# One load each for w_up and wo, all heads normalized at once, and w_down cut at half rows 16 and 24, in a decode kernel on one core

## The chip, the cores and the metric

The kernel runs on one core of one Trainium2 chip. The metric is the device time of one execution in microseconds (us); lower is better. The core has a matmul engine (TensorE, PE in the profile, its weight loads as PEld), VectorE (DVE), ScalarE (ACT), GpSimd (POOL) and SyncE (SP), which here issues nearly all DMAs. Sixteen DMA engines serve the core.

## The reference

One token passes through an attention block and a gated MLP, in bfloat16. All weights and caches are read once.

```python
# D = 640, Hq = Hkv = 32, Sk = 4096, Dh = 128, Df = 1728; B = S = 1
def _A_ref(x, k_cache, v_cache, wq, wo):            # x is layernormed
    q = (x @ wq)                                    # [640] -> 32 heads x 128
    scores = einsum("bhqd,bhkd->bhqk", q, k_cache) * (Dh ** -0.5)
    p = softmax(scores)
    o = einsum("bhqk,bhkd->bhqd", p, v_cache)
    return o.reshape(B, Sq, Hq * Dh) @ wo           # [4096] -> [640]

def _B_ref(x, w_gate, w_up, w_down):                # x is layernormed
    return (gelu(x @ w_gate) * (x @ w_up)) @ w_down # 640 -> 1728 -> 640

h  = x + _A_ref(layernorm(x), k_cache, v_cache, wq, wo)
h2 = h + _B_ref(layernorm(h), w_gate, w_up, w_down)
```

The key and value caches are 33.5 MB each, the weights 17 MB together: 84.2 MB in all.

## The kernel before, in words

The instructions of each engine are written out by hand. A small class (`Prog`) keeps one list per engine in program order and turns the dependencies given with each operation into semaphore waits. There is no scheduler: an engine runs its list in order, and where its next operation waits, all behind it wait too. SP issues every load from one list, so the loads also queue in program order on the same 16 DMA engines.

**Attention.** The 32 heads are handled in four groups `G` of 8. A group's keys come as one 8.4 MB load to one of three slots: 128 partitions, 16 for each head, with 256 keys each. The values come the same way. The order is K0, V0, K1, V1, K2, K3, V2, V3, and a slot is loaded again when its reader is done. For each group, eight times (`c`): VectorE multiplies keys with the query (`score_mult`, L310), PE folds the products with eight identity matmuls (L318 and L30), VectorE sums (`score_sum`, L327). Then `softmax` (L332 to L341), `attend` (64 matmuls of probabilities with values, L353), and `pick` (L359 to L363), which brings the group's output to `po_r`. `head_sum` (L367, L369) adds over the 16 partitions of a head; its results collect in bank 4 (`ps_a`).

**Normalize, spread, take.** Heads go in two halves, `t`: `t=0` is groups 0 and 1, `t=1` groups 2 and 3. `normalize(t)` divides by the softmax sums (L373, L374), `spread(t)` is one matmul (L377) that lays 16 heads out over 128 partitions eight times, and `take(t)` keeps the wanted one of eight and adds up (L381, L386). The result, `aP[:, t, :]`, is a column for each of 16 rows of wo that a partition holds. For `t=0` this runs inside group 2's loop (at `c` = 4, 5 and 6), for `t=1` after the last `attend`.

**Projection.** wo comes in two loads, `d_wo[0]` and `d_wo[1]`, each 16 rows to a partition (20,480 bytes). `proj_part(t, lo, hi)` does two matmuls for each row (L398 and, with weights kept, L30), four rows side by side in 32-column strips of the array. All of `t=0` stands in PE's list ahead of `d_wo[1]`'s matmuls, woven between `head_sum(3)` and `spread(1)`.

**Tail.** The projected row is cast to a high and a low part (L471 to L473), turned to columns (L479), added to x and layernormed (L272 to L282, L488, L489). `glu` (L512) is 20 matmuls for the gate, then 20 for up: 12 on the first w_up load (`d_wu[0]`, three of five row blocks), 8 on the second. `turn` casts a row of results (L518, VectorE for the gate, ScalarE for up) and turns it to columns by six matmuls (L522, L524). VectorE and ScalarE compute gelu (L535 to L542) and the product `hm` (L545, L547). `down` is 54 matmuls (L555, L564), two for each of w_down's 27 half rows of 320 elements on 128 partitions; they come in three loads cut at `LOADS`. Two casts (L567) and the output DMA follow.

**Padding.** `run_on(n)` (L455, L30) puts n matmuls of an identity, 512 columns wide, into PE's list, whose result nobody reads. They stand at the places where PE would idle in the tail.

SP's list at the end, in order: wo (two loads, waiting for `attend(2)`), w_gate (waiting for group 3's last fold), w_up (two), w_down (three), output.

Of the kernel before, what the change touches and what calls it, by code (L numbers as in the profile page):

```python
# [5 lines left out]
FP32 = mybir.dt.float32  # L6
BF16 = mybir.dt.bfloat16
ALU = mybir.AluOpType
# [3 lines left out]
D = 640  # L12
# [10 lines left out]
PIECE = 320  # L23
LOADS = ((0, 19), (19, 25), (25, 27))

# [86 lines left out]
def bass_sequential_preLN__gqa_block_cached__glu_gated_geglu__decode_kernel(nc, A_x, A_k_cache, A_v_cache, A_wq, A_wo, B_x, B_w_gate, B_w_up, B_w_down, out):  # L112
# [16 lines left out]
    hlnT = sb("hlnT", [128, 5], BF16)  # L129
    rz = sb("rz", [16, 2], FP32)  # L130
    po_r = sb("po_r", [128, 2, DH + 1], FP32)
    m4 = sb("m4", [128, 4], FP32)
    hs = sb("hs", [128, 24], FP32)
    hb = sb("hb", [128, 24], FP32)
    hbx = sb("hbx", [128, 8, 4], BF16)
    aT = sb("aT", [16, 2, 128], BF16)
    aP = sb("aP", [128, 2, 16], BF16)
    sel = sb("sel", [16, 16, 8], BF16)
    m8 = sb("m8", [128, 8], FP32)
    aM = sb("aM", [128, 8, 16], FP32)  # L140
    sel4 = sb("sel4", [128, 4], BF16)
# [31 lines left out]
    hs_t = first_t.take(128).rearrange("p (a b c) -> p a b c", a=8, b=4)  # L173
    m8_t = first_t.take(128).rearrange("p (a b) -> p a b", a=8)
    par_t = first_t.take(128).rearrange("p (a b) -> p a b", a=2)
# [18 lines left out]
    wq_sb = slots[2][:, 0:5 * 4096]  # L194
    wo_sb = slots[0][:, 0:32 * D].rearrange("p (t i n) -> p t i n", t=2, i=16)
    wg_sb = slots[2][:, 0:5 * DF].rearrange("p (c n) -> p c n", c=5)
# [44 lines left out]
    c_bz = GP(lambda e: e.memset(hb[:, :], 0.0))  # L241
    c_hb = mask(hb[:, 8:16], ones_b[:, 0:8], [[-16, 8]], 0, 1, ALU.is_ge, c_bz)
    c_hb = mask(hb[:, 8:16], hb[:, 8:16], [[16, 8]], 15, -1, ALU.is_ge, c_hb)
    c_m4 = mask(m4_t, ones_b[:, 0:128].rearrange("p (a b) -> p a b", a=4), [[-1, 4], [-4, 32]], 0, 1, ALU.is_equal)
# [5 lines left out]
    c_hx = mask(hbx[:, :, :], hbx[:, :, :], [[16, 8], [0, 4]], 15, -1, ALU.is_ge, c_hx)  # L250
    c_sel = mask(sel[:, :, :], ones_b[0:16, 0:128].rearrange("p (a b) -> p a b", a=16), [[1, 16], [0, 8]], 0, -1, ALU.is_equal)
    c_m8 = mask(m8_t, ones_b[:, 0:128].rearrange("p (a b) -> p a b", a=8), [[-1, 8], [-8, 16]], 0, 1, ALU.is_equal)

    c_odd = V(lambda e: e.reduce_sum(odd[:, :], hb[:, 8:16].rearrange("p (a b) -> p b a", b=2), axis=AX.X), c_hb)
    c_far = V(lambda e: e.tensor_scalar(far[:, :, :], odd[:, :].unsqueeze(2).to_broadcast([128, 2, 16]), -1e38, 1e38, ALU.mult, ALU.add), c_odd)
    c_m4 = V(lambda e: e.reduce_sum(m4[:, :], m4_t, axis=AX.X), c_m4)
    c_m8 = V(lambda e: e.reduce_sum(m8[:, :], m8_t, axis=AX.X), c_m8)
    c_hs = V(lambda e: e.reduce_sum(hs[:, 8:16], hs_t.rearrange("p a b c -> p a (b c)"), axis=AX.X), c_hs, c_hz)
    c_o4 = V(lambda e: e.reduce_max(ones4[:, :], sel4[:, :], axis=AX.X), c_s4)
# [37 lines left out]
    q1 = V(lambda e: e.tensor_copy(qb[:, :, :].rearrange("p g d -> p (g d)"), ps_q[:, :]), qd)  # L297
    free2 = [qd, c_par, c_m4, c_m8, c_hs, c_idb]

    folds, reds, exps, pbs, pvs, mks, evs, hds, nbs = {}, {}, {}, {}, {}, {}, {}, {}, {}  # L300
    z4s, spr, aPs = {}, {}, {}
    held = [False]

    def other(fn, *d):
        held[0] = False
        return T(fn, *d)
# [58 lines left out]
    def head_sum(G):  # L365
        g, at = G % 2, 132 * (G // 2)
        other(lambda e: e.matmul(ps_a[0:16, at + DH:at + DH + 1], hb[:, 8 - 8 * g:24 - 8 * g], po_r[:, g, DH:DH + 1],  # L367
                                 start=(g == 0), stop=(g == 1), skip_group_check=True), exps[G], z4s.get(G // 2 - 1), c_hb)
        hds[G] = T(lambda e: e.matmul(ps_a[0:16, at:at + DH], hs[:, 8 - 8 * g:24 - 8 * g], po_r[:, g, 0:DH],  # L369
                                      start=False, stop=(g == 1), skip_group_check=True), evs[G], c_hs)  # L370

    def normalize(t):
        rc = V(lambda e: e.reciprocal(rz[:, t:t + 1], ps_a[0:16, 132 * t + DH:132 * t + DH + 1]), hds[2 * t + 1])  # L373
        z4s[t] = V(lambda e: e.tensor_scalar(aT[:, t, :], ps_a[0:16, 132 * t:132 * t + DH], rz[:, t:t + 1], None, ALU.mult), rc)  # L374

    def spread(t):
        spr[t] = other(lambda e: e.matmul(ps_z[:, 32:160], sel[:, :, :].rearrange("p a b -> p (a b)"), aT[:, t, :], start=True, stop=True),  # L377
                       z4s[t], c_sel)

    def take(t):  # L380
        m = V(lambda e: e.tensor_tensor(out=aM[:, :, :], in0=ps_z[:, 32:160].rearrange("p (q i) -> p q i", q=8),  # L381
                                        in1=m8[:, :].unsqueeze(2).to_broadcast([128, 8, 16]), op=ALU.mult), spr[t], c_m8)

        def fn(e):
            with nc.allow_low_precision(reason="one of the eight terms is not zero"):
                return e.reduce_sum(aP[:, t, :], aM[:, :, :].rearrange("p q i -> p i q"), axis=AX.X)  # L386
        aPs[t] = V(fn, m)

    def proj_part(t, lo, hi, *ws):
        def fn(e):  # L390
            for i4 in range(lo, hi, 4):
                for half in range(2):
                    for i in range(i4, i4 + 4):
                        a = 32 * (i - i4)
                        args = (bank[half][a:a + 1, 0:320], aP[:, t, i:i + 1], wo_sb[:, t, i, 320 * half:320 * half + 320])
                        start, stop = t == 0 and i < 4, t == 1 and i >= 12
                        if half == 0:
                            r = e.matmul(*args, start=start, stop=stop)  # L398
                        else:
                            r = matmul_again(nc, *args, start, stop, (128, 32), (0, a))  # L400
            return r
        return T(fn, *ws)

    PARTS = 4
    for G in range(NG):
        for c in range(8):
            if c == 5 and G == 3:
                attend(2)
            score_mult(G, c)
            if c >= 1:  # L410
                score_sum(G, c - 1)
            if c == 1 and G in (1, 2):
                pick(G - 1)
            if c == 3 and G in (1, 2):
                head_sum(G - 1)
            if c == 4 and G == 2:
                normalize(0)
            if c == 5 and G == 2:
                spread(0)
            if c == 6 and G == 2:  # L420
                take(0)
            if c == 7 and G == 3:
                pick(2)
        score_sum(G, 7)
        softmax(G)
        if G == 0:
            load("K", 1, *free2)
            load("V", 1, done[("K", 0)])
        if G == 3:
            head_sum(2)  # L430
        if G != 2:
            attend(G)
        if G == 0:
            load("K", 2, done[("V", 0)])
        if G == 1:
            load("K", 3, done[("K", 1)])
            load("V", 2, done[("V", 1)])
        if G == 2:
            load("V", 3, done[("K", 2)])


    d_wo = [P.dma("sync", wo_sb[:, t, :, :], A_wo[2048 * t:2048 * t + 2048, :].rearrange("(p i) n -> p i n", i=16), done[("V", 2)])
            for t in range(2)]
    free = done[("K", 3)]
    wu_v = B_w_up[:, :].rearrange("(p c) n -> p c n", c=5)
# [154 lines left out]
```

## Time and profile before

| | us |
|---|---|
| median of 3 runs | 202.11 (201.89 to 202.12) |
| the profiled execution: its time | 201.88 |
| its span, from first to last instruction | 200.6 |
| outside the span | 1.28 |

| engine | busy, us | share of the span |
|---|---|---|
| DVE | 117.7 | 59% |
| PE | 108.5 | 54% |
| PEld | 17.3 | 9% |
| ACT | 6.5 | 3% |
| POOL | 3.5 | 2% |

The loads moved 84.32 MB in the span, 420 GB/s. The slices of the page show the busy share of each engine in 40 equal stretches of 5.0 us, PEclk the clock that was granted to TensorE in tenths of full speed. The chain of waits follows the work that ended last, back from the last instruction. A timeline line has the start, the busy time, the engine, the line of the kernel and the tiles; in brackets stand the idle time ahead of it and what ended that. The last loads, with the time from issue to landing:

| load | size, KB | issued | landed after, us |
|---|---|---|---|
| wo, two | 2560 each | 163.6, 164.0 | 13.3, 19.1 |
| w_gate | 2160 | 170.3 | 17.9 |
| w_up, two | 1296, 864 | 170.6, 171.1 | 20.6, 22.3 |
| w_down, three | 1520, 480, 160 | 171.6, 172.0, 172.5 | 25.4, 26.1, 26.0 |

### The profile page before, as it was taken

What the parts mean: (1) busy time and instruction counts of PE and PEld (TensorE: products, weight loads), DVE (VectorE), ACT (ScalarE), POOL (GpSimd) and SP (SyncE); (2) the same over time, 40 slices, a digit from 0 to 9 for tenths busy, and PEclk for the clock granted to TensorE, in tenths of its full rate; (3) what the DMA queues carried; (4) which work ended last, traced back from release to release, by engine and by line L of the source; (5) the groups of instructions that cost most, each with busy time, mean ns of one, the idle gap of its engine ahead of it and who ended that gap; (6) DMA issues with size and microseconds to landing.
All of it is one profiled execution on the core that took longest, in us unless ns stands there. A gap on an engine that the chain in (4) does not pass through costs nothing.

```text
span 200.6 us, 1537 instructions
## 1 busy us (share of the span) xinstructions
PE 108.5 (54%) x792; PEld 17.3 (9%) x501; DVE 117.7 (59%) x157; ACT 6.5 (3%) x17; POOL 3.5 (2%) x18
## 2 busy tenths in 40 slices
PE   0108000676666108587637093856085897487884
PEld 0103000000003000000012000000000020132323
DVE  3200001799974027989860479997879969534240
ACT  2010000000001000000010000000100000100110
POOL 7000000000000000000000000000000000000000
PEclk9999755599999955879997679999669999799999
DMA  9999999999999999999999999999999999999992
GB/s 359 417 479 418 418 418 418 418 431 470 536 431 418 397 431 431 418 431 418 418 418 418 434 536 444 418 418 418 444 418 418 431 418 389 429 421 436 405 421 100
DMA packets 2460, 84.32 MB, mean 420 GB/s; under 512 B 275, under 2 KB 406, under 8 KB 662
## 3 DMA queue, kind: packets, MB, share of 16 engines
q1 hardware_dynamic: 2452, 84.23, 97.7%
q8 instruction: 5, 0.08, 0.2%
q14 instruction: 1, 0.01, 0.0%
q10 hardware_dynamic: 2, 0.00, 0.0%
HBM read 84.23 MB, written 0.00 MB: 420 GB/s over the span
## 4 chain that ended last, share of the span: by engine, by line
DMA 53%; DVE 30%; PE 14%; issue 1%; SPq 1%; ACT 1%
DMA slot<-in_A_k_cache_dram 40%; DVE slot L310 21%; DMA slot<-in_B_w_down_dram 13%; PE bank L30 9%; DVE sc L327 6%; PE bank L353 4%; PE bank L555 1%; DVE mix L341 1%; SPq L61 1%; PE bank L318 1%; DVE mx L332 0%; ACT p_t L337 0%; DVE mix L359 0%; DVE mxd L333 0%; DVE mxd L335 0%
## 5 line engine op out<-in xcount | busy, mean ns | idle before, releaser
L310 DVE TENSOR_TENSOR slot<-slot,qb 128x4096 bf16<-128x4096 bf16 x32 | 72.7, 2283 | 32.9 <-DMA slot<-in_A_k_cache_dram 32.9
L30 PE MATMUL bank<-slot,id_b 128*128 128x512 bf16 x249 | 65.6, 415 | 27.6 <-DVE slot L310 27.6
L327 DVE TENSOR_REDUCE sc<-bank 128x32 f32<-128x512 f32 x32 | 22.0, 686 | 11.8 <-PE bank L30 11.8
L318 PE MATMUL bank<-slot,id_b 128*128 128x512 bf16 x7 | 3.4, 483 | 35.7 <-DVE slot L310 35.7
L353 PE MATMUL bank<-slot,mix 128*32 128x512 bf16 x256 | 17.7, 440 | 8.8 <-DVE mix L341 8.8
L353 PEld LDWEIGHTS bank<-slot,mix 128*32 128x32 bf16 x256 | 7.3, 109 | 74.9 <-DVE mix L341 41.6
L293 PE MATMUL bank<-slot,xlnM 128*32 128x512 bf16 x40 | 4.3, 612 | 5.7 <-DMA slot<-in_A_wq_dram 5.7
L341 DVE TENSOR_TENSOR mix<-p_t,hbx 128x512 bf16<-128x512 bf16 x16 | 5.7, 421 | 2.7 <-ACT p_t L337 2.7
L337 ACT ACTIVATE p_t<-sc,nb 128x256 bf16<-128x256 f32 x4 | 2.0, 508 | 159.6 <-DVE nb L336 159.6
L297 DVE CAST qb<-bank 128x512 bf16<-128x512 f32 x1 | 0.7, 692 | 8.5 <-PE bank L293 8.5
L359 DVE TENSOR_TENSOR mix<-bank,m 128x512 f32<-128x512 f32 x4 | 2.7, 683 | 4.2 <-PE bank L353 4.2
L266 PE MATMUL bank<-one_bf,x_keep 1*128 1x1 bf16 x5 | 0.4, 177 | 8.3 <-DMA x_keep<-in_A_x_dram 8.3
L455 PE MATMUL bank<-id_b 128*128 128x512 bf16 x11 | 4.2, 384 | 0.0
L512 PE MATMUL bank<-slot,hlnT 128*1 128x512 bf16 (+1 forms) x40 | 3.8, 476 | 0.5 <-DMA slot<-in_B_w_up_dram 0.4
L318 PEld LDWEIGHTS bank<-slot,id_b 128*128 128x128 bf16 x7 | 0.7, 99 | 38.6 <-DVE slot L310 38.1
L367 PEld LDWEIGHTS bank<-po_r,hb 128*16 128x16 f32 x8 | 0.4, 94 | 32.2 <-issue 32.2
L30 PE MATMUL bank<-id_b 128*128 128x512 bf16 x10 | 3.1, 378 | 0.0
L398 PE MATMUL bank<-slot,aP 128*1 128x320 bf16 x32 | 2.5, 298 | 0.5 <-DMA slot<-in_A_wo_dram 0.5
L555 PE MATMUL bank<-slot,hm 128*2 128x160 bf16 x52 | 2.0, 232 | 1.1 <-DMA slot<-in_B_w_down_dram 1.1
L30 PE MATMUL bank<-slot,aP 128*1 128x320 bf16 x32 | 2.5, 298 | 0.0
L567 DVE CAST slot<-bank 2x160 bf16<-2x160 f32 x1 | 0.3, 311 | 3.5 <-PE bank L564 3.5
L293 PEld LDWEIGHTS bank<-slot,xlnM 128*32 128x32 bf16 x40 | 1.6, 139 | 7.7 <-issue 7.7
(94 smaller groups left out, 42.1 us busy)
## 6 DMA issues: line engine op xcount, KB each, us to landing
slot<-in_A_wq_dram SPq DMA_DIRECT2D x1, 5120.0 KB, 15.2
slot<-in_A_wo_dram SPq DMA_DIRECT2D x2, 2560.0 KB, 16.2
slot<-in_B_w_gate_dram SPq DMA_DIRECT2D x1, 2160.0 KB, 17.9
slot<-in_B_w_down_dram SPq DMA_DIRECT2D x1, 1520.0 KB, 25.4
slot<-in_B_w_up_dram SPq DMA_DIRECT2D x1, 1296.0 KB, 20.6
slot<-in_B_w_up_dram SPq DMA_DIRECT2D x1, 864.0 KB, 22.3
slot<-in_B_w_down_dram SPq DMA_DIRECT2D x1, 480.0 KB, 26.1
slot<-in_B_w_down_dram SPq DMA_DIRECT2D x1, 160.0 KB, 26.0
```

The lines of the kernel that those rows point to most:

```text
L30: return e.add_instruction(mybir.InstMatmult(name=nc.get_next_instruction_name(), engine=e.engine, start_tensor_calc=start, stop_tensor_ca ...
L293: i = e.matmul(ps_q[32 * j:32 * j + 32, :], xlnM[:, 160 * s + 32 * c:160 * s + 32 * c + 32], wq_j[:, c, 2 * j + s, :, :], start=(c == 0 an ...
L310: m = V(lambda e: e.tensor_tensor(out=kt, in0=kt, in1=qb[:, G, :].unsqueeze(1).to_broadcast([128, 32, DH]), op=ALU.mult), landed[("K", G)] ...
L318: i = e.matmul(*args, start=True, stop=False)
L327: reds[(G, c)] = V(lambda e: e.reduce_sum(sc[:, 32 * c:32 * c + 32], ps_f[c % 2][:, :].rearrange("p (g d) -> p g d", d=16), axis=AX.X), fo ...
L341: pbs[(G, n)] = pbs[G] = V(lambda e, lo=lo, hi=hi: e.tensor_tensor(out=p_bd[:, lo:hi, :].rearrange("p c (a r) -> p c a r", a=8), in0=p_t[: ...
L353: i = e.matmul(po[a:a + 32, 0:512], p_bd[:, c, :], vt[:, 4 * c:4 * c + 4, :], start=(c < 4), stop=(c >= 60))
L359: mks[G] = V(lambda e: e.tensor_tensor(out=po_m, in0=po[:, 0:512].rearrange("p (b d) -> p b d", b=4), in1=m4[:, :].unsqueeze(2).to_broadca ...
L398: r = e.matmul(*args, start=start, stop=stop)
L455: i = e.matmul(*args, start=True, stop=True)
L512: i = e.matmul(po[32 * a:32 * a + 1, 512 * k:512 * k + 128 * n], hlnT[:, c:c + 1], cols, start=(c == 0), stop=(c == 4))
L555: i = e.matmul(ps_d[32 * t:32 * t + 2, :], hm[:, at:at + 2], wd_sb[:, PIECE * c + 160 * t:PIECE * c + 160 * t + 160], start=False, stop=(c ...
```

## The change

wo comes as one load, 32 rows to a partition (40,960 bytes), and w_up as one. The halves `t` are gone: `head_sum` collects all four groups in one 32-row result, and `normalize`, `spread` and `take` run once, after the last `attend`, for 32 heads; group 2's loop loses its three steps. `spread` now lays 32 heads out four times, and `take` keeps one of four, so the mask `m8` is not needed. All 64 projection matmuls stand in one piece behind the one wo load, with `run_on(3)`, `run_on(1)` and `run_on(6)` ahead of them in place of the woven `t=0` parts, `run_on(1)` and `run_on(4)`. Up's 20 matmuls stand in one piece behind the one w_up load and behind the gate's `turn`; the `run_on` between is 6 in place of 3. w_down's loads are cut at half rows 16 and 24 in place of 19 and 25.

```diff
-LOADS = ((0, 19), (19, 25), (25, 27))
+LOADS = ((0, 16), (16, 24), (24, 27))
...
-    rz = sb("rz", [16, 2], FP32)
+    rz = sb("rz", [32, 1], FP32)
...
-    aP = sb("aP", [128, 2, 16], BF16)
-    sel = sb("sel", [16, 16, 8], BF16)
-    m8 = sb("m8", [128, 8], FP32)
-    aM = sb("aM", [128, 8, 16], FP32)
+    aT = sb("aT", [32, 128], BF16)
+    aP = sb("aP", [128, 32], BF16)
+    sel = sb("sel", [32, 32, 4], BF16)
+    aM = sb("aM", [128, 4, 32], FP32)
...
     def head_sum(G):
-        g, at = G % 2, 132 * (G // 2)
-        other(lambda e: e.matmul(ps_a[0:16, at + DH:at + DH + 1], hb[:, 8 - 8 * g:24 - 8 * g], po_r[:, g, DH:DH + 1],
-                                 start=(g == 0), stop=(g == 1), skip_group_check=True), exps[G], z4s.get(G // 2 - 1), c_hb)
-        hds[G] = T(lambda e: e.matmul(ps_a[0:16, at:at + DH], hs[:, 8 - 8 * g:24 - 8 * g], po_r[:, g, 0:DH],
-                                      start=False, stop=(g == 1), skip_group_check=True), evs[G], c_hs)
...
+        lo = 24 - 8 * G
+        other(lambda e: e.matmul(ps_a[0:32, DH:DH + 1], hb[:, lo:lo + 32], po_r[:, G % 2, DH:DH + 1],
+                                 start=(G == 0), stop=(G == 3), skip_group_check=True), exps[G], c_hb)
+        hds[G] = T(lambda e: e.matmul(ps_a[0:32, 0:DH], hs[:, lo:lo + 32], po_r[:, G % 2, 0:DH],
+                                      start=False, stop=(G == 3), skip_group_check=True), evs[G], c_hs)
+
+    def normalize():
+        rc = V(lambda e: e.reciprocal(rz[:, :], ps_a[0:32, DH:DH + 1]), hds[3])
+        return V(lambda e: e.tensor_scalar(aT[:, :], ps_a[0:32, 0:DH], rz[:, 0:1], None, ALU.mult), rc)
...
+    def proj(e):
+        for i4 in range(0, 32, 4):
+            for half in range(2):
+                for i in range(i4, i4 + 4):
+                    a = 32 * (i - i4)
+                    args = (bank[half][a:a + 1, 0:320], aP[:, i:i + 1], wo_sb[:, i, 320 * half:320 * half + 320])
+                    if half == 0:
+                        r = e.matmul(*args, start=(i < 4), stop=(i >= 28))
+                    else:
+                        r = matmul_again(nc, *args, i < 4, i >= 28, (128, 32), (0, a))
+        return r
...
-            if c == 4 and G == 2:
-                normalize(0)
-            if c == 5 and G == 2:
-                spread(0)
-            if c == 6 and G == 2:
-                take(0)
...
-    d_wo = [P.dma("sync", wo_sb[:, t, :, :], A_wo[2048 * t:2048 * t + 2048, :].rearrange("(p i) n -> p i n", i=16), done[("V", 2)])
-            for t in range(2)]
+    d_wo = P.dma("sync", slots[0][:, 0:32 * D], A_wo[:, :].rearrange("(p i) n -> p (i n)", i=32), done[("V", 2)])
...
-    d_wu = [P.dma("sync", wu_sb[:, 0:3, :], wu_v[:, 0:3, :]),
-            P.dma("sync", wu_sb[:, 3:5, :], wu_v[:, 3:5, :])]
+    d_wu = P.dma("sync", wu_sb, B_w_up[:, :].rearrange("(p c) n -> p c n", c=5))
...
     pick(NG - 1)
-    proj_part(0, 0, 8, aPs[0], d_wo[0], reds[(NG - 1, 7)])
+    run_on(3)
+    head_sum(NG - 1)
+    z = normalize()
     run_on(1)
-    head_sum(NG - 1)
-    normalize(1)
-    proj_part(0, 8, 12)
-    spread(1)
-    take(1)
-    proj_part(0, 12, 16)
-    run_on(4)
-    pr = proj_part(1, 0, 16, aPs[1], d_wo[1])
+    sp = spread(z)
+    pw = take(sp)
+    run_on(6)
+    pr = T(proj, pw, d_wo, reds[(NG - 1, 7)])
...
     ga = T(glu(0, 0, range(5)), hl, d_wg, mks[NG - 1])
     run_on(2)
-    T(glu(1, 5 * DF, range(3)), d_wu[0], c_po)
     ga = turn(0, ps_g, ga)
-    run_on(3, ps_s[:, :])
-    up = T(glu(1, 5 * DF, range(3, 5)), d_wu[1])
+    run_on(6, ps_s[:, :])
+    up = T(glu(1, 5 * DF, range(5)), d_wu, c_po)
     run_on(2, ps_s[:, :])
```

More of the change, by code (lines that the diff above doesn't have):

```diff
@@ L129, in bass_sequential_preLN__gqa_block_cached__glu_gated_geglu__decode_kernel @@
     hlnT = sb("hlnT", [128, 5], BF16)
-    rz = sb("rz", [16, 2], FP32)
+    rz = sb("rz", [32, 1], FP32)
     po_r = sb("po_r", [128, 2, DH + 1], FP32)
     m4 = sb("m4", [128, 4], FP32)
-    hs = sb("hs", [128, 24], FP32)
-    hb = sb("hb", [128, 24], FP32)
+    hs = sb("hs", [128, 56], FP32)
+    hb = sb("hb", [128, 56], FP32)
     hbx = sb("hbx", [128, 8, 4], BF16)
-    aT = sb("aT", [16, 2, 128], BF16)
-    aP = sb("aP", [128, 2, 16], BF16)
-    sel = sb("sel", [16, 16, 8], BF16)
-    m8 = sb("m8", [128, 8], FP32)
-    aM = sb("aM", [128, 8, 16], FP32)
+    aT = sb("aT", [32, 128], BF16)
+    aP = sb("aP", [128, 32], BF16)
+    sel = sb("sel", [32, 32, 4], BF16)
+    aM = sb("aM", [128, 4, 32], FP32)
     sel4 = sb("sel4", [128, 4], BF16)
@@ L173, in bass_sequential_preLN__gqa_block_cached__glu_gated_geglu__decode_kernel @@
     hs_t = first_t.take(128).rearrange("p (a b c) -> p a b c", a=8, b=4)
-    m8_t = first_t.take(128).rearrange("p (a b) -> p a b", a=8)
     par_t = first_t.take(128).rearrange("p (a b) -> p a b", a=2)
@@ L194, in bass_sequential_preLN__gqa_block_cached__glu_gated_geglu__decode_kernel @@
     wq_sb = slots[2][:, 0:5 * 4096]
-    wo_sb = slots[0][:, 0:32 * D].rearrange("p (t i n) -> p t i n", t=2, i=16)
+    wo_sb = slots[0][:, 0:32 * D].rearrange("p (i n) -> p i n", i=32)
     wg_sb = slots[2][:, 0:5 * DF].rearrange("p (c n) -> p c n", c=5)
@@ L241, in bass_sequential_preLN__gqa_block_cached__glu_gated_geglu__decode_kernel @@
     c_bz = GP(lambda e: e.memset(hb[:, :], 0.0))
-    c_hb = mask(hb[:, 8:16], ones_b[:, 0:8], [[-16, 8]], 0, 1, ALU.is_ge, c_bz)
-    c_hb = mask(hb[:, 8:16], hb[:, 8:16], [[16, 8]], 15, -1, ALU.is_ge, c_hb)
+    c_hb = mask(hb[:, 24:32], ones_b[:, 0:8], [[-16, 8]], 0, 1, ALU.is_ge, c_bz)
+    c_hb = mask(hb[:, 24:32], hb[:, 24:32], [[16, 8]], 15, -1, ALU.is_ge, c_hb)
     c_m4 = mask(m4_t, ones_b[:, 0:128].rearrange("p (a b) -> p a b", a=4), [[-1, 4], [-4, 32]], 0, 1, ALU.is_equal)
@@ L250, in bass_sequential_preLN__gqa_block_cached__glu_gated_geglu__decode_kernel @@
     c_hx = mask(hbx[:, :, :], hbx[:, :, :], [[16, 8], [0, 4]], 15, -1, ALU.is_ge, c_hx)
-    c_sel = mask(sel[:, :, :], ones_b[0:16, 0:128].rearrange("p (a b) -> p a b", a=16), [[1, 16], [0, 8]], 0, -1, ALU.is_equal)
-    c_m8 = mask(m8_t, ones_b[:, 0:128].rearrange("p (a b) -> p a b", a=8), [[-1, 8], [-8, 16]], 0, 1, ALU.is_equal)
-    c_odd = V(lambda e: e.reduce_sum(odd[:, :], hb[:, 8:16].rearrange("p (a b) -> p b a", b=2), axis=AX.X), c_hb)
+    c_sel = mask(sel[:, :, :], ones_b[0:32, 0:128].rearrange("p (a b) -> p a b", a=32), [[1, 32], [0, 4]], 0, -1, ALU.is_equal)
+    c_odd = V(lambda e: e.reduce_sum(odd[:, :], hb[:, 24:32].rearrange("p (a b) -> p b a", b=2), axis=AX.X), c_hb)
     c_far = V(lambda e: e.tensor_scalar(far[:, :, :], odd[:, :].unsqueeze(2).to_broadcast([128, 2, 16]), -1e38, 1e38, ALU.mult, ALU.add), c_odd)
     c_m4 = V(lambda e: e.reduce_sum(m4[:, :], m4_t, axis=AX.X), c_m4)
-    c_m8 = V(lambda e: e.reduce_sum(m8[:, :], m8_t, axis=AX.X), c_m8)
-    c_hs = V(lambda e: e.reduce_sum(hs[:, 8:16], hs_t.rearrange("p a b c -> p a (b c)"), axis=AX.X), c_hs, c_hz)
+    c_hs = V(lambda e: e.reduce_sum(hs[:, 24:32], hs_t.rearrange("p a b c -> p a (b c)"), axis=AX.X), c_hs, c_hz)
     c_o4 = V(lambda e: e.reduce_max(ones4[:, :], sel4[:, :], axis=AX.X), c_s4)
@@ L297, in bass_sequential_preLN__gqa_block_cached__glu_gated_geglu__decode_kernel @@
     q1 = V(lambda e: e.tensor_copy(qb[:, :, :].rearrange("p g d -> p (g d)"), ps_q[:, :]), qd)
-    free2 = [qd, c_par, c_m4, c_m8, c_hs, c_idb]
+    free2 = [qd, c_sel, c_par, c_m4, c_hs, c_idb]
     folds, reds, exps, pbs, pvs, mks, evs, hds, nbs = {}, {}, {}, {}, {}, {}, {}, {}, {}
-    z4s, spr, aPs = {}, {}, {}
     held = [False]
@@ L372, in normalize @@
[L372 to L382, printed above, removed]
-        def fn(e):
-            with nc.allow_low_precision(reason="one of the eight terms is not zero"):
-                return e.reduce_sum(aP[:, t, :], aM[:, :, :].rearrange("p q i -> p i q"), axis=AX.X)
-        aPs[t] = V(fn, m)
@@ L389, in proj_part @@
[L389 to L402, printed above, removed]
+        lo = 24 - 8 * G
@@ new lines, in spread, with take @@
+    def spread(z):
+        return T(lambda e: e.matmul(ps_z[:, 32:160], sel[:, :, :].rearrange("p a b -> p (a b)"), aT[:, :], start=True, stop=True), z, c_sel)
+    def take(sp):
+        m = V(lambda e: e.tensor_tensor(out=aM[:, :, :], in0=ps_z[:, 32:160].rearrange("p (q i) -> p q i", q=4),
+                                        in1=m4[:, :].unsqueeze(2).to_broadcast([128, 4, 32]), op=ALU.mult), sp, c_m4)
+        def fn(e):
+            with nc.allow_low_precision(reason="one of the four terms is not zero"):
+                return e.reduce_sum(aP[:, :], aM[:, :, :].rearrange("p q i -> p i q"), axis=AX.X)
+        return V(fn, m)
@@ L439, in bass_sequential_preLN__gqa_block_cached__glu_gated_geglu__decode_kernel @@
             load("V", 3, done[("K", 2)])
-    d_wo = [P.dma("sync", wo_sb[:, t, :, :], A_wo[2048 * t:2048 * t + 2048, :].rearrange("(p i) n -> p i n", i=16), done[("V", 2)])
-            for t in range(2)]
+    d_wo = P.dma("sync", slots[0][:, 0:32 * D], A_wo[:, :].rearrange("(p i) n -> p (i n)", i=32), done[("V", 2)])
     free = done[("K", 3)]
-    wu_v = B_w_up[:, :].rearrange("(p c) n -> p c n", c=5)
     wd_v = B_w_down[:, :].rearrange("(p2 r) n -> p2 (r n)", r=27).rearrange("p2 (s f) -> (p2 s) f", s=2)
     d_wg = P.dma("sync", wg_sb, B_w_gate[:, :].rearrange("(p c) n -> p c n", c=5), free)
-    d_wu = [P.dma("sync", wu_sb[:, 0:3, :], wu_v[:, 0:3, :]),
-            P.dma("sync", wu_sb[:, 3:5, :], wu_v[:, 3:5, :])]
+    d_wu = P.dma("sync", wu_sb, B_w_up[:, :].rearrange("(p c) n -> p c n", c=5))
     d_wd = [P.dma("sync", wd_sb[:, PIECE * lo:PIECE * hi], wd_v[:, PIECE * lo:PIECE * hi]) for lo, hi in LOADS]
```

## The prediction

> **What bounds the kernel now.** I read first the slices and the chain shares on the page, to see which engine the span hangs on.
>
> ```profile
> DMA  9999999999999999999999999999999999999992
> ...
> DMA 53%; DVE 30%; PE 14%; issue 1%; SPq 1%; ACT 1%
> ```
>
> The 16 DMA engines are over 90% busy in 39 of 40 slices: the loads run end to end, and no byte is added or removed. So the question is only how much work stands behind the landings at the end. The chain of waits, in order of time, shows its last steps:
>
> ```profile
> 171.59 25.39 DMA slot<-in_B_w_down_dram
> 196.97 0.04 issue
> 197.02 1.96 PE bank L555 x52
> 198.98 0.11 PE bank L564 x2
> ```
>
> The largest w_down load lands at 196.97, and all 54 matmuls run behind it without a pause. The other two loads land at 198.1 and 198.5 (issues at 172.0 and 172.5 plus 26.1 and 26.0 us), just ahead of their matmuls. Next I read the timeline of the last 18 us, to see how close the computation is behind the loads (columns: start, us, engine, line; in brackets the idle time and who ended it).
>
> ```profile
> 183.14 0.31 PE L398 MATMUL bank<-slot,aP 128*1 128x320 bf16 x4 [0.54 <-DMA slot<-in_A_wo_dram]
> ...
> 188.61 1.80 PE L512 MATMUL bank<-slot,hlnT 128*1 128x512 bf16 x20
> ...
> 193.41 0.81 PE L512 MATMUL bank<-slot,hlnT 128*1 128x512 bf16 x8
> ...
> 194.27 0.59 ACT L518 CAST slot<-bank 97x512 bf16<-97x512 f32 x1 [0.34 <-PE bank L512]
> ...
> 195.33 0.59 PE L30 MATMUL bank<-id_b 128*128 128x512 bf16 x2
> ...
> 197.02 1.96 PE L555 MATMUL bank<-slot,hm 128*2 128x160 bf16 x52 [1.10 <-DMA slot<-in_B_w_down_dram]
> ```
>
> Loads hold the PE in turn: the second wo load (0.54 us), the second w_up load (landed 193.4, matmuls at 193.41) and the first w_down load (1.10 us). From wo's landing a serial path runs: projection, columns, layernorm, gate, up, hm. It reaches w_down with 1.1 us of PE to spare, and that slack is what this change draws on.
>
> **The change part by part.** *Stages ahead of 183 us.* With t=0 no longer normalized in group 2, DVE loses 0.44 us (L373, L374 from 129.18 to 129.62) and 0.59 us (135.22 to 135.81), about 1.03 us, where it is the bound; scores of groups 2 and 3 end up to 1.0 us earlier. That gives nothing at the end: it issues wo and the B loads up to 1.0 us earlier into a queue which V's last load keeps full until 170.8, and wo was issued at 163.6. What is late next is the queue itself. The same normalization for all heads (recip 0.16, scale 0.34, spread 0.23, mask 0.29, reduce 0.37, with hops 1.6 us from po_r) follows the last attend as t=1's does: aP was ready at 182.0, and is ready between 181.0 and 182.0, under wo's landing at 183.0. If that cover were gone it would cost what it overran. The masks' start-up change (m8 gone, sel 32 wide) lies before the first matmuls: nothing.
>
> *The merged loads.* From the trace's packets by size, a 40,960-byte row took 1.514 us and two 20,480-byte rows 2 x 0.764; at 8 rows per DMA engine that is 0.11 us less for wo, by landings rather 0.08. For w_up 17,280 bytes took 0.644 against 0.389 + 0.262: 0.06 by packets, 0.09 by landings. I take 0.08 and 0.09 (bounds 0 and 0.15 each). wo then lands at 182.93, w_up at 193.2, the last w_down load at 198.34. SP issues two loads fewer (0.43 us each), hidden by 20 us of queue.
>
> The Trainium skill, DMA: Bandwidth & Descriptors, section Anatomy of one DMA, puts a fixed cost of about 2 us on a DMA, by which, as time on the stream, the sum with two loads fewer would come out some 4 us lower (an estimate from that page). The trace disagrees for queued loads: 160 KB more landed 0.4 us after its predecessor.
>
> *The projection.* This is the main term. Before, half of the 64 matmuls ran ahead of the landing; behind it stood 8 groups of 4, of which the first began at 183.14 and the last at 184.09: 0.135 us a group. After, all 16 groups wait. Landing 182.93, the same 0.13 us of wait and weight load, first group at 183.06, last at 183.06 + 15 x 0.135 = 185.09; the cast (L471, L472) starts 0.35 behind, at 185.44 against 184.44: **+1.00 us**. Everything to the gate is unchanged in order and moves with it: 188.61 becomes 189.61 (w_gate landed at 188.1).
>
> *Gate, turn, up.* Before, w_up's first 12 matmuls filled the DVE cast of the gate row; after, PE waits for that cast (L518 on DVE, 190.46, 0.69 us). Gate 189.61, its cast 1.85 later at 191.46, over at 192.15, turn matmuls at 192.21. Then run_on is 6 in place of 3: six at 0.216 from 192.42, and 0.10 to change over (as at 187.18 to 187.49), so up starts at 193.81. w_up landed 0.6 us before, so the padding, not the load, is what it waits for. All 20 up matmuls now run here as the gate's did, 1.85 to the cast: ACT at 195.66 against 194.27, **+1.39 us**. Cast 0.59, turn at 196.30, hm 0.64 after that; but run_on(3) behind the turn (0.205 + 3 x 0.216 + 0.10) frees PE later, at 197.25. The gelu chain ends by 194.5 and is hidden.
>
> *w_down.* Its first load is 16 rows of 640 bytes on 128 partitions instead of 19: 0.246 MB less at 427 GB/s, 0.575 us earlier, 196.98 - 0.575 - 0.17 = 196.23. That is ready a microsecond before PE is: the split gains nothing any more. PE starts at 197.25 against 197.02. Loads two and three land at about 197.76 and 198.34; their matmuls come at 197.25 + 32 x 0.0346 = 198.36 and 198.91. No wait, so the end moves with the start: **+0.23 us**.
>
> Sum: 1.00 from the projection and 0.39 more by the padding and up make 1.39 at the ACT cast. From that cast to a free PE it is 1.59 us (195.66 to 197.25), so before, PE was free at 194.27 + 1.59 = 195.86 and idled 1.16 until 197.02. 1.39 - 1.16 = 0.23. The profiled execution took 201.88 us (span 200.6); 202.11 for it, and on the median of 202.11, which lies 0.23 above that execution, **202.34 us**. With merge savings at their ends (0 or 0.15 on wo) it is 0.31 or 0.16; the change-over of 0.10 could be 0 or 0.3 at three places, so -0.1 to +0.8 at the far ends, and 0 to 0.5 as the likely spread: 202.1 to 202.6.
>
> **The rivals.** *The clock.* After the last attend PE is padded less: four 512-wide matmuls and the head sum, then six, then 1.1 to 1.5 us idle until 183.06. The trace's granted clock changes only at steps of 3.41 us. PE in some of these windows (columns: window, its length, PE busy with its count, granted clock, then DMA):
>
> ```profile
> 60.30:63.71 3.41, 1.51 (x28) 1.00 0.75 327
> 80.78:84.19 3.41, 1.36 (x7) 1.00 1.24 538
> 84.20:87.61 3.41, 3.41 (x9) 0.50 0.84 365
> 138.81:142.22 3.41, 1.15 (x6) 1.00 1.24 538
> 142.23:145.63 3.40, 0.00 (x0) 0.50 0.80 347
> 179.77:183.18 3.41, 2.27 (x27) 1.00 0.99 423
> ```
>
> 1.51 us busy was followed by the full clock (63.71 on), 1.36 and 1.15 by 0.50. The window that showed 2.27 here would have 1.7 to 2.2 with the new order: over the point. But if the windows fall otherwise and the last attend runs at full clock, so ends two us sooner, the padding is spent by 180.4 and the window before the landing has about 0.7 us. Then up to all 16 projection groups take 0.27 in place of 0.135. That is up to +2.0 us, half of it when the window ends inside: 203.3, slower. It decides at 1.4 us busy of the last 3.41. For it: less padding. Against: most positions of the window hold 1.6 or more.
>
> The Trainium skill, TensorE: Matmul & The Clock Gate, Part 1, lets the clock fall only after an idle window of some 3.4 us; by that there is no such risk here, but the 1.36 us above were followed by 0.50 without a window idle.
>
> *A fixed cost per load.* If each queued load costs up to 0.4 us of stream, as the smallest one's landing allows, wo lands 0.4 earlier, not 0.08: 0.32 less, 202.02. The even rate of wo's halves (2.62 MB in 6.1 us, 430 GB/s, like the long loads) speaks against.
>
> *The last landing sets the end.* If the path had 0.5 us less than I count (padding cheaper, cast overlapped), PE would be caught up and the end would be 198.34 + 0.04 + 6 matmuls: last start 198.55 against 198.82, 201.84. Two summed steps would have to be wrong.
>
> *The change does not act:* if wo's wait did not gate the first half, 202.1. In the changed kernel's order of instructions one wait stands ahead of all 64 matmuls.
>
> **How the numbers follow.** A measurement of this kernel can tell about 0.2% (0.40 us) from no change: 201.71 to 202.51 is "same". Forecast mechanism 0.72, of which 0.44 inside that band and 0.28 above it (its errors are mostly additional hops); clock 0.15, slower; fixed cost 0.06 (0.04 same, 0.02 faster); last landing 0.05 (0.03, 0.02); no action 0.02, same. Faster 0.04, same 0.53, slower 0.43. Range: from the fixed-cost and upper part of the landing case, 201.9, to the middle of the clock case, 203.1; beyond lie some 0.08 above and 0.07 below.
>
> **What would show it.** After: wo one landing near 182.9, PE's first projection group right behind it and its last 2.0 us later; the gate at 189.6; up's matmuls starting behind run_on and not behind a DMA; PE before w_down ending its idle time on PE or DVE, not on the DMA; 54 matmuls without a pause. Wrong if PE still waits for w_down at 197 (last-landing case), if the clock reads 0.5 between 180 and 188 (clock case), or if wo lands before 182.7 (fixed cost).

## The result and the profile after

| | before, us | changed, us |
|---|---|---|
| median, 21 runs of each | 202.04 (201.75 to 202.25) | 202.34 (202.02 to 203.06) |
| the profiled execution | 201.88 | 202.82 |
| its span | 200.6 | 201.6 |

The medians differ by 0.30 us. The ratio, taken over all runs, is 1.0020 (95% interval 1.0014 to 1.0027), which is 0.4 us, since the upper times weigh in it: a small difference, but not zero. The changed kernel's times also lie much further apart: 12 of the 21 between 202.02 and 202.36, and 9 between 202.50 and 203.06, where before had none over 202.25. The profiled execution is one of the nine. (Of the kernel a_up_two below, the profiled execution was a disturbed one of 236.73 us, so none of its lines are shown.)

The page's shares of the chain, then the chain in order of time (start, us, what) of the changed kernel's profiled execution:

```profile
DMA 49%; DVE 29%; PE 19%; issue 1%; ACT 1%; SPq 0%
```

```profile
162.88 19.95 DMA slot<-in_A_wo_dram
182.83 0.14 issue
182.97 0.31 PE bank L390 x4
...
189.96 2.21 PE bank L492 x8
192.17 0.02 issue
192.19 0.70 DVE slot L498
...
193.52 1.08 PE bank L30 x5
194.60 1.74 PE bank L492 x14
...
197.59 0.43 PE bank L30 x2
198.02 1.89 PE bank L534 x52
```

w_down has left the chain. The last DMA on it is now wo, landed at 182.83, and from there to the output it is computation without a gap, with the padding (L30 x5) on it. The timeline shows the steps that the prediction timed:

```profile
182.97 0.31 PE L390 MATMUL bank<-slot,aP 128*1 128x320 bf16 x4 [2.47 <-DMA slot<-in_A_wo_dram]
...
185.35 0.49 DVE L451 CAST slot<-bank 97x320 bf16<-97x320 f32 x1 [5.52 <-PE bank L30]
...
189.89 2.25 PE L492 MATMUL bank<-slot,hlnT 128*1 128x512 bf16 x20
...
194.53 1.79 PE L492 MATMUL bank<-slot,hlnT 128*1 128x512 bf16 x20
...
197.95 1.96 PE L534 MATMUL bank<-slot,hm 128*2 128x160 bf16 x52
```

The gate's 20 matmuls took 2.25 us, up's 20 took 1.79. The stretches between the steps of the granted clock tell why (window, length, PE busy with its count, granted clock, then DMA share and GB/s):

```profile
181.63:185.04 3.41, 2.07 (x64) 1.00 0.98 421
185.05:188.45 3.40, 2.58 (x27) 1.00 0.99 417
188.47:191.87 3.40, 3.40 (x33) 0.50 0.98 418
191.88:195.28 3.40, 3.13 (x29) 1.00 0.99 414
```

From 188.47 to 191.87 TensorE ran at half clock. That is the end of the layernorm stage and most of the gate.

### The profile page after: what moved, and what is told of

Same layout as the page of the kernel before. It is cut to its first block, busy times and chain, and to the rows that moved or that the text cites. A ratio compares the mean times of both kernels' runs of the same rounds, so it can differ in the third digit from the quotient of the medians.

```text
span 201.6 us, 1537 instructions
## 1 busy us (share of the span) xinstructions
PE 111.9 (56%) x799; PEld 17.7 (9%) x500; DVE 116.5 (58%) x152; ACT 6.5 (3%) x17; POOL 3.4 (2%) x17
## 4 chain that ended last, share of the span: by engine, by line
DMA 49%; DVE 29%; PE 19%; issue 1%; ACT 1%; SPq 0%
DMA slot<-in_A_k_cache_dram 39%; DVE slot L305 20%; DMA slot<-in_A_wo_dram 10%; PE bank L30 9%; DVE sc L322 5%; PE bank L348 4%; PE bank L492 2%; PE bank L534 1%; DVE mix L336 1%; PE bank L390 1%; PE bank L437 1%; PE bank L313 1%; PE bank L477 0%; DVE slot L453 0%; DVE mx L327 0%
## 5 line engine op out<-in xcount | busy, mean ns | idle before, releaser
L30 PE MATMUL bank<-slot,id_b 128*128 128x512 bf16 x250 | 66.8, 419 | 26.5 <-DVE slot L305 26.4
L313 PE MATMUL bank<-slot,id_b 128*128 128x512 bf16 x6 | 3.0, 498 | 33.5 <-DVE slot L305 33.5
L437 PE MATMUL bank<-id_b 128*128 128x512 bf16 x12 | 4.8, 402 | 0.0
L30 PE MATMUL bank<-id_b 128*128 128x512 bf16 x17 | 4.8, 379 | 0.0
L451 DVE CAST slot<-bank 97x320 bf16<-97x320 f32 x1 | 0.5, 491 | 5.5 <-PE bank L30 5.5
L390 PE MATMUL bank<-slot,aP 128*1 128x320 bf16 x32 | 2.2, 299 | 2.5 <-DMA slot<-in_A_wo_dram 2.5
L362 PEld LDWEIGHTS bank<-po_r,hb 128*32 128x32 f32 x8 | 0.6, 108 | 31.9 <-issue 31.9
L498 DVE CAST slot<-bank 97x512 bf16<-97x512 f32 x1 | 0.7, 692 | 2.7 <-PE bank L492 2.7
L30 PE MATMUL bank<-slot,aP 128*1 128x320 bf16 x32 | 2.2, 299 | 0.0
```

The costliest lines, as they stand in the source:

```text
L30: return e.add_instruction(mybir.InstMatmult(name=nc.get_next_instruction_name(), engine=e.engine, start_tensor_calc=start, stop_tensor_ca ...
L313: i = e.matmul(*args, start=True, stop=False)
L390: r = e.matmul(*args, start=(i < 4), stop=(i >= 28))
L437: i = e.matmul(*args, start=True, stop=True)
```

## The experiments

Theory S: the serial path from wo's landing has used up its slack of 1.1 us, so everything on it shows at the end. Theory C: windows at half clock behind 172 us make up the upper times. The rivals are the loads (their merging and cuts), normalizing all heads at once, and padding that pays for itself. All ratios are to the kernel before, run beside them.

### The changed kernel again

> The changed kernel once more, beside the next ones on the same chip. All theories: a median of 202.2 to 202.4, about a third of the times above 202.45.

Measured: 202.21 us (202.02 to 203.02, 12 runs) against 202.06, ratio 1.0011 (1.0002 to 1.0020). Two of 12 were over 202.45; with the first set it is 11 of 33. Of 97 runs of the kernel before beside these experiments, one was (202.61). The profiled execution, 202.19 us, had the full clock from 177 us on, and so shows theory S by itself:

```profile
183.15 0.31 PE L390 MATMUL bank<-slot,aP 128*1 128x320 bf16 x4 [0.84 <-DMA slot<-in_A_wo_dram]
...
189.70 1.78 PE L492 MATMUL bank<-slot,hlnT 128*1 128x512 bf16 x20
...
193.87 1.81 PE L492 MATMUL bank<-slot,hlnT 128*1 128x512 bf16 x20
...
195.73 0.59 ACT L498 CAST slot<-bank 97x512 bf16<-97x512 f32 x1 [1.93 <-PE bank L492]
...
197.32 1.96 PE L534 MATMUL bank<-slot,hm 128*2 128x160 bf16 x52
```

The gate takes 1.78 us here. PE comes to w_down at 197.32, 0.30 behind the 197.02 of before; the time is 0.31 above.

### wo in two loads again, heads still normalized at once

```diff
-    def proj(e):
+    def proj(e, lo, hi):
...
-    d_wo = P.dma("sync", slots[0][:, 0:32 * D], A_wo[:, :].rearrange("(p i) n -> p (i n)", i=32), done[("V", 2)])
+    wo_v = A_wo[:, :].rearrange("(p i) n -> p i n", i=32)
+    d_wo = [P.dma("sync", wo_sb[:, 16 * t:16 * t + 16, :], wo_v[:, 16 * t:16 * t + 16, :], done[("V", 2)]) for t in range(2)]
...
-    run_on(6)
-    pr = T(proj, pw, d_wo, reds[(NG - 1, 7)])
+    run_on(4)
+    T(lambda e: proj(e, 0, 16), pw, d_wo[0], reds[(NG - 1, 7)])
+    run_on(1)
+    pr = T(lambda e: proj(e, 16, 32), d_wo[1])
```

> The changed kernel with wo in two loads again (rows 0 to 15 and 16 to 31 of each partition), one normalization for all heads kept; the first 32 projection matmuls stand ahead of the second load. Theory S (a serial path from wo's landing has lost its slack; the projection behind the landing is 1.0 us of it): the last projection group starts near 184.1 and not 185.0, the path is 0.9 us shorter, PE is free for w_down near 196.8, and the last w_down landing sets the end: 0.2 us below the kernel before, 201.8 to 202.0. Rival N (normalizing all heads at once is what costs, not the one load): as the changed kernel, 202.3. Rival L (the loads themselves, their cuts and merging, moved the time): at most 0.1 us from the changed kernel.

Measured: 201.80 us (201.67 to 201.97, 11 runs), ratio 0.9989 (0.9980 to 0.9998). The change minus its one wo load is faster than before, so rival N falls: normalizing at once costs nothing that shows. Rival L falls too: the last w_down load landed at 198.61 here, later than the 198.33 of the changed kernel, and the time was shorter all the same. The chain starts from another load:

```profile
169.78 23.63 DMA slot<-in_B_w_up_dram
193.41 0.04 issue
193.45 1.81 PE bank L495 x13
```

This execution had half clock as well, in the gate (2.30 us for its 20 matmuls), and took 201.87 us all the same. The slack ahead of w_up's landing hid it.

```profile
188.63 2.30 PE L495 MATMUL bank<-slot,hlnT 128*1 128x512 bf16 x20
...
191.94 0.38 PE L438 MATMUL bank<-id_b 128*128 128x512 bf16 x1
192.16 1.24 PE L30 MATMUL bank<-id_b 128*128 128x512 bf16 x5
193.45 1.78 PE L495 MATMUL bank<-slot,hlnT 128*1 128x512 bf16 x20
```

The chain doesn't show waits shorter than a matmul's recorded 0.23 us, as the matmuls of w_down start 0.035 us apart and so overlap. By the start of each, PE stood twice more: at the second load, which landed at 198.04, and at the third, which landed at 198.61 and let the last six matmuls start at 198.66. So the last landing set the end, as theory S said.

### w_up in two loads again

```diff
-    d_wu = P.dma("sync", wu_sb, B_w_up[:, :].rearrange("(p c) n -> p c n", c=5))
+    wu_v = B_w_up[:, :].rearrange("(p c) n -> p c n", c=5)
+    d_wu = [P.dma("sync", wu_sb[:, 0:3, :], wu_v[:, 0:3, :]),
+            P.dma("sync", wu_sb[:, 3:5, :], wu_v[:, 3:5, :])]
...
-    ga = turn(0, ps_g, ga)
-    run_on(6, ps_s[:, :])
-    up = T(glu(1, 5 * DF, range(5)), d_wu, c_po)
+    T(glu(1, 5 * DF, range(3)), d_wu[0], c_po)
+    ga = turn(0, ps_g, ga)
+    run_on(3, ps_s[:, :])
+    up = T(glu(1, 5 * DF, range(3, 5)), d_wu[1])
```

> The changed kernel with w_up in two loads again, 12 of up's 20 matmuls ahead of the gate's turn and run_on 3 behind it. Theory S: up's end comes 0.9 us earlier (8 matmuls and 3 padding matmuls behind the turn in place of 20 and 6), PE is free for w_down near 196.4, the last landing sets the end: 0.2 us below the kernel before, 201.8 to 202.0. Rival N (normalizing at once) and rival L (loads): as the changed kernel, 202.3.

Measured: 201.94 us (201.73 to 202.16, the ten executions beside the profiled one), ratio 1.0000 (0.9991 to 1.0009). Giving back either part of the serial work undoes the change's loss. The gain of 0.2 that theory S wanted isn't seen: the medians differ by 0.05, and the interval allows 0.18. No profile shows why.

### The padding ahead of up, less and more

```diff
-    run_on(6, ps_s[:, :])
+    run_on(3, ps_s[:, :])      # a_pad3; run_on(9, ...) in a_pad9
```

> The changed kernel with run_on(3) in place of run_on(6) between the gate's turn and up. Theory S (the padding stands on the path): up starts when w_up lands or 0.65 us earlier than it did, PE is free 0.5 to 0.65 us earlier, 201.8 to 202.0 in executions at full clock. Theory C (the clock: half-rate windows in the stage from 184 to 192 make up the upper third of the changed kernel's times): the upper times stay, 0.5 to 0.9 us above the lower ones. Rival P (the padding is what keeps the clock up, taking it away costs): no gain or slower, 202.3 or more.

> The changed kernel with run_on(9) in place of run_on(6) between the gate's turn and up. Theory S (nothing behind the gate has slack left): the three matmuls of 0.216 us come out at the end in full, 0.65 us more than the changed kernel: 202.8 to 203.0. Rival P (padding there keeps the clock up and so pays for part of itself): 202.3 to 202.6.

Measured: with 3, 201.91 us (201.72 to 202.49, 11 runs), ratio 0.9999 (0.9990 to 1.0007); with 9, 202.93 us (202.66 to 203.58, 6 runs), ratio 1.0049 (1.0037 to 1.0061). Three matmuls more cost 0.65 us of TensorE and moved the median by 0.59 over 202.34 and by 0.72 over 202.21. Three fewer gave 0.30 to 0.43: in the profile of that kernel up waits for w_up instead, which landed at 193.24, and PE then stands 0.09 and 0.04 us longer than its pace for w_down's second and third loads. Rival P falls. Theory C had wanted the upper third of the times to stay with 3; one of 11, 202.49, lies apart. The slack won back may hide the others; no run shows it.

### w_down's old cuts in the changed kernel, the new ones in the kernel before

```diff
-LOADS = ((0, 16), (16, 24), (24, 27))
+LOADS = ((0, 19), (19, 25), (25, 27))      # a_loads_old; the reverse in b_loads_new
```

> The changed kernel with w_down cut at half rows 19 and 25 again. Theory S (PE comes to w_down only at 197.1 to 197.25): the first load lands near 196.8, still ahead of PE, so nothing changes: 202.2 to 202.4. Rival L (the cuts are what costs): back to 202.0.

> The kernel before with w_down cut at half rows 16 and 24. Theory S: PE is free at 195.9, the first load lands 0.57 earlier (196.4), the last landing at 198.5 and six matmuls behind it set the end: 0.1 us lower, 201.85 to 202.0. Rival L (the cuts are what costs in the change): 202.2 or more.

Measured: the old cuts in the changed kernel gave 202.36 us (202.00 to 202.91, 12 runs, six over 202.45), ratio 1.0019 (1.0008 to 1.0029): no difference, as S said. The new cuts in the kernel before gave 202.05 us (201.74 to 202.40, 11 runs), ratio 0.9997 (0.9988 to 1.0005). The gain of 0.1 isn't seen. In its profile PE stood at the first and at the second load:

```profile
196.66 1.27 PE L555 MATMUL bank<-slot,hm 128*2 128x160 bf16 x32 [0.57 <-DMA slot<-in_B_w_down_dram]
198.20 0.91 PE L555 MATMUL bank<-slot,hm 128*2 128x160 bf16 x20 [0.28 <-DMA slot<-in_B_w_down_dram]
```

PE took the first 32 matmuls as soon as they could go, then waited until 198.20 with 22 still to do. By the start of each matmul it stood once more, until 198.80, for the third load, so the last six set the end, as I had counted. What I had wrong is when that load lands: at 198.76 and not at 198.5. V's last load landed 0.09 us later here than in the profile of before. And the three w_down loads take longer with the new cuts: from w_up's landing on the first of the 16 engines to the last load's it was 5.27 us in this kernel and in the changed one, and 5.17 with the old cuts in either.

### One w_up load in the kernel before

```diff
-    d_wu = [P.dma("sync", wu_sb[:, 0:3, :], wu_v[:, 0:3, :]),
-            P.dma("sync", wu_sb[:, 3:5, :], wu_v[:, 3:5, :])]
+    d_wu = P.dma("sync", wu_sb, B_w_up[:, :].rearrange("(p c) n -> p c n", c=5))
...
-    T(glu(1, 5 * DF, range(3)), d_wu[0], c_po)
     ga = turn(0, ps_g, ga)
-    run_on(3, ps_s[:, :])
-    up = T(glu(1, 5 * DF, range(3, 5)), d_wu[1])
+    run_on(6, ps_s[:, :])
+    up = T(glu(1, 5 * DF, range(5)), d_wu, c_po)
```

> The kernel before with w_up as one load, up's 20 matmuls behind the gate's turn and run_on 6. Theory S: up ends 1.0 us later, PE is free for w_down at about 196.85, about when the first w_down load lands (196.9): the slack of 1.1 us is used up and the time stays, 201.95 to 202.15, but windows at half clock behind 184 us, which the slack hid, now show: single times up to 202.6. Rival U (one w_up alone makes the whole of the loss): 202.3.

Measured: 202.00 us (201.78 to 202.28, 11 runs), ratio 0.9996 (0.9988 to 1.0005). The same work that is 0.39 us on the changed kernel's path is free here. The chain still ends with w_down:

```profile
170.94 26.02 DMA slot<-in_B_w_down_dram
196.95 0.04 issue
197.00 1.96 PE bank L552 x52
```

PE's last padding matmul made way for the next at about 196.7. Of the slack of 1.1 us about 0.2 was left, and nothing showed. The single times up to 202.6 that I expected from half clock did not come.

### Padding against the half clock

```diff
-    run_on(1)                  # four places of the layernorm stage:
+    run_on(2)                  # a_lnpad, a_fullpad, a_allpad
...
-    run_on(6)                  # ahead of the projection:
+    run_on(10)                 # a_fullpad; run_on(14) in a_allpad
...
         if G == 3:
             head_sum(2)
+            run_on(8)          # a_allpad alone, ahead of the last attend
```

> The changed kernel with one more padding matmul at each of four places of the layernorm stage where PE idles (run_on 2 in place of 1 around both column steps, ahead of the mean and behind the residual). Theory C (the changed kernel's upper third, 202.5 to 203.06, comes from windows at half clock in this stage and the gate): all times lie at 202.0 to 202.4 and no profile shows 0.5 between 184 and 192; the median falls by 0.1. Theory S alone: no change, or up to 0.1 more where padding delays a step; the spread stays 1 us. Rival L (the spread comes from the loads): the spread stays.

> The changed kernel with the layernorm stage padded as in a_lnpad, and run_on(10) in place of run_on(6) ahead of the projection. Theory C2 (a_lnpad's two times over 203 come from a projection at half clock, after a window in which PE idled ahead of wo's landing): they go, all times at 202.1 to 202.45. Rival: they come from elsewhere, and times over 203 stay, about 2 in 11. Theory S: the median stays at 202.27, as the padding is spent before wo lands.

> The changed kernel with the padded layernorm stage, run_on(8) ahead of the last attend and run_on(14) ahead of the projection, so that PE idles at most 1 us at any place between 169 and 185 us. Theory C (all times above 202.45 come from windows at half clock behind 172 us): the last attend always runs at full clock, nothing behind it at half, all times at 202.1 to 202.45, none near 203. Rival R (the times near 203 have another cause, such as a DMA engine's lateness): about 2 in 10 stay near 203. Theory S: median 202.2 to 202.3 either way.

| kernel | median, us | range | over 202.45 | ratio |
|---|---|---|---|---|
| changed, both sets | 202.34, 202.21 | 202.02 to 203.06 | 11 of 33 | 1.0020, 1.0011 |
| a_lnpad | 202.27 | 202.16 to 203.33 | 2 of 11 | 1.0020 (1.0008 to 1.0032) |
| a_fullpad | 202.23 | 202.16 to 203.08 | 3 of 11 | 1.0022 (1.0010 to 1.0034) |
| a_allpad | 202.19 | 201.94 to 202.39 | 0 of 11 | 1.0008 (0.9999 to 1.0017) |

With the layernorm stage padded, none of 22 times lies between 202.41 and 202.97, where the changed kernel had 9 of 33. The closest comparison is a_loads_old, which does the same work in that stage and ran beside a_fullpad: 6 of 12 against none of 11, by chance about once in 110 times. The profiles fit: in those of the changed kernel (202.82) and of a_wo_two the last attend ran at full clock and the gate at half; in that of a_fullpad the last attend ran at full clock too, PE was 3.21 us busy in the window of the layernorm stage (184.36 to 187.75) in place of 2.58 and 2.71, and the clock stayed full.

But five times lie from 202.98 up. My theory for those, a half clock in the projection after idling ahead of wo, fell with a_fullpad: more padding there left them. With padding ahead of the last attend too they are gone, but that is weaker: against the 5 of 22, none of 11 would come up by chance about once in 9 times, and against the changed kernel run beside it (2 of 12 over 202.45) all upper times would be missing once in 4. So that the half clock makes the group between 202.5 and 202.9 is well supported; what makes the times near 203 isn't settled, as no profile caught one.

The profiled a_allpad execution had the full clock from 148 us on:

```profile
179.10:182.50 3.40, 2.63 (x13) 1.00 0.97 415
182.50:185.90 3.40, 2.84 (x66) 1.00 1.01 432
185.93:189.33 3.40, 3.22 (x33) 1.00 1.03 432
189.35:192.74 3.39, 3.12 (x32) 1.00 0.98 415
```

### A version that beats both

wo and w_up in two loads each as above, one normalization, and w_down in four loads, the last of one half row:

```diff
-LOADS = ((0, 16), (16, 24), (24, 27))
+LOADS = ((0, 16), (16, 23), (23, 26), (26, 27))
...
         dn = T(lambda e, t=t: e.matmul(ps_d[32 * t:32 * t + 2, :], hm[:, 0:2], wd_sb[:, PIECE * 26 + 160 * t:PIECE * 26 + 160 * t + 160],
-                                       start=False, stop=True))
+                                       start=False, stop=True), d_wd[3])
```

> One normalization for all heads, as in the changed kernel, but wo and w_up in two loads each, and w_down in four, cut at half rows 16, 23 and 26. Theory S: PE is free for w_down before its first load lands (195.5 to 196), and the last landing near 198.4 with two matmuls behind it sets the end: 0.2 to 0.3 us below the kernel before, 201.7 to 201.85, spread under 0.4 us. Rival L (each more load costs 0.1 us or more): 202.0.

Measured: 201.76 us (201.54 to 202.29, 11 runs), ratio 0.9986 (0.9977 to 0.9994). PE waits for w_down again:

```profile
195.23 0.59 PE L30 MATMUL bank<-id_b 128*128 128x512 bf16 x2
196.39 2.34 PE L540 MATMUL bank<-slot,hm 128*2 128x160 bf16 x52 [0.56 <-DMA slot<-in_B_w_down_dram]
198.56 0.24 PE L549 MATMUL bank<-slot,hm 128*2 128x160 bf16 x2
```

The time came out as forecast, the end of the path not quite. By the start of each matmul PE stood at the second load (landed 197.69) and at the third (198.31), which held the last eight matmuls; the fourth, at 198.51, was just in time for its two. The spread is 0.75 us, where I had expected under 0.4. And against a_wo_two (ratio 0.9989) the four loads have no gain that these runs can tell.

## Why the prediction was right, and where not

**The sum.** Right in place and nearly in size: 0.23 us forecast, 0.30 and 0.15 measured as medians, 0.31 in the profiled execution at full clock. In that execution each step stands 0.06 to 0.09 behind its forecast, all of it from wo's landing (183.01, forecast 182.93):

| step | forecast, us | full clock | half clock |
|---|---|---|---|
| first projection group | 183.06 | 183.15 | 182.97 |
| cast of the projected row | 185.44 | 185.53 | 185.35 |
| gate | 189.61 | 189.70 | 189.89 |
| cast of the gate row | 191.46 | 191.53 | 192.19 |
| up | 193.81 | 193.87 | 194.53 |
| PE comes to w_down | 197.25 | 197.32 | 197.95 |

**Luck in the number.** That the median came out at the forecast 202.34 to the hundredth is luck. The forecast started from 202.11, the median of three runs of the kernel before, where 21 gave 202.04. And the median holds a third of upper times, which the sum doesn't contain: the 12 lower ones of the 21 have a median of 202.22, 0.18 above before, and a_allpad, which has no upper ones, stands 0.13 above. So at full clock the medians give 0.13 to 0.18 for the serial path. The 0.31 is the difference of two single executions, of which that of before was 0.16 under its median.

**The projection** was the main term, 1.00 us; between its first group and the last 2.03 us passed in both profiles, as 15 x 0.135. a_wo_two took it out again and fell to 201.80.

**Up and its padding**, 0.39 us: a_pad9 shows that the padding counts in full, a_pad3 that it does so until the landings of w_up and w_down take over, and b_up_one that all of it is free where slack is left.

**w_down's cuts** were worth nothing here, as said (a_loads_old). But they aren't free on the stream, as the next paragraph shows.

**The merged loads.** Forecast 0.08 and 0.09 us. By the first of the 16 engines to land, wo took 12.13 us after V's last load in place of 12.19, and w_up 5.12 after w_gate in place of 5.22. But the three w_down loads took 5.27 in place of 5.17, so only 0.05 of the 0.17 was left at the last landing. It is the new cuts that cost the 0.10: a_loads_old took 5.17, b_loads_new 5.27. I had counted them as free; with PE late it made no difference here.

**The clock rival** was the step that I mis-sized. I gave it 0.15, placed it ahead of the projection, and let it decide at 1.4 us busy in 3.41. Its condition came about in the profile after: the last attend ran at full clock, the padding was spent by 180.5, and PE stood 2.47 us ahead of wo's landing. Yet the clock stayed full behind the two windows there, with 1.97 us busy (178.23 to 181.62) and 2.07. Half clock came in the gate, from 188.47, just behind the stretch from 180 to 188 that the prediction named as the sign, and behind a window that had been 2.58 us busy; in a_wo_two it followed one with 2.71. Before had 2.69 and kept the full clock. The windows of a_wo_two, then those of before:

```profile
184.88:188.28 3.40, 2.71 (x29) 1.00 1.05 447
188.30:191.70 3.40, 3.36 (x23) 0.50 0.94 403
...
183.20:186.59 3.39, 2.69 (x45) 1.00 1.00 418
186.60:190.00 3.40, 3.15 (x37) 1.00 1.00 422
```

So the busy time doesn't tell the cases apart, and 1.4 us is no limit. It counts a matmul of one column (L459) at 0.18 us, one of 512 columns (L437) at 0.38, and the 27 matmuls of the window ahead of the gate are mostly columns, layernorm and residual. That the clock weighs such small matmuls less is my reading; no run shows it by itself.

A third of the times (11 of 33) lie 0.3 to 0.9 us above the median of the others. By the table, the half clock of the one that was profiled cost 0.81 us between wo's first group and w_down. The price that I gave, up to 2.0 us and 1.0 as the likely figure, was too high: at half clock were the gate and the end of the layernorm stage, and not the projection.

The Trainium skill, TensorE: Matmul & The Clock Gate, Part 1, asks for an idle window before the clock falls; 2.58 of 3.40 us busy ahead of the 0.50 speaks against that as a limit. It also calls the window free-running, not reset by a kernel's start. The traces agree: the clock's steps lie at 172.94 and 176.36 in the profile of before, and at 188.47 and 191.87 in that after, which is 15.53 us or 4.55 windows on, and so not at the same place of a window. That would fit with executions of one kernel falling into two groups; no run shows that it is the cause.

**The rivals that fell.** A fixed cost per load: each of the two merges saved the stream 0.1 us or less, where this rival wanted up to 0.4. The 2 us in the Trainium skill, DMA: Bandwidth & Descriptors, section Anatomy of one DMA, are given there for DMAs of GpSimd, and mostly as latency of completion. SyncE issues these loads, and what the landings here show is their time on the stream, so they don't contradict that page; no run here measures such a latency. The last landing: even at full clock PE came to w_down 0.9 us after its first load had landed (196.40), and its last six matmuls started 0.46 us after the last landing (198.52). Where PE came earlier, in a_wo_two, a_pad3 and b_loads_new, the last landing did set the end.

## What to carry to other kernels

Before splitting or merging a load, ask how much work its one wait holds back, and how much slack the path behind it has up to the next landing. Here, in the profiles at full clock, 1.46 us of added path (ACT's cast of up at 195.73 in place of 194.27) cost 0.30, since 1.16 us had stood free ahead of w_down; work added to that path now would cost in full, as the padding of a_pad9 did. Slack at the end also hides what varies, such as a window at half clock: when a change uses it up, look at the spread of the times, not only at the median.

## What the runs showed of the hardware

The clock fell to half behind windows in which the profile had PE 76% and 80% busy with small matmuls, and in the first of these two executions it stayed full behind one with 61%, of projection matmuls; four more 512-column matmuls over the layernorm stage, 0.86 us of streaming, took the group of times between 202.5 and 202.9 away. And one load's shares on the 16 engines land far apart: for the last w_down load 196.64 for the first and 198.33 for the last in the changed kernel, so that 1.7 us at the end of the stream lie between the earliest and the latest engine, and six of the 16 landed after 197.7. No run here tells why.
